# Weight conversions held behind an attention factor, a block of one chunk's input taken from SBUF, and two loads issued later, in a fused attention and two-layer expert kernel

## The chip, the cores and the metric

The kernel runs on one core of a Trainium2 chip. The metric is device time in microseconds (us) of one execution. The core has engines that run side by side, each through its own queue and in that queue's order: TensorE (PE, with its weight loads shown apart as PEld), VectorE (DVE), ScalarE (ACT), GpSimd (POOL), and SyncE (SP), whose queue here issues all the DMA transfers. An instruction that waits holds back everything behind it on its engine.

## What is computed

An attention with a memory term over 4 batches, 8 heads, 576 tokens and a head size of 64 gives 2304 tokens of 512 features; these go through a gated layer and then through a second layer. Cut to what matters:

```python
scores = q @ k.T / 8, causal;  a = softmax(scores);  local = a @ v
q_p = where(q > 0, q, exp(q) - 1) + 1
mem = (q_p @ M_prev) / (q_p @ z_prev + 1e-6)
x = g * mem + (1 - g) * local              # g = sigmoid(beta), per head
x = (sigmoid(x @ w_gate) * (x @ w_val)) @ w_out      # 512 -> 1536 -> 512
h = x @ w_in                                          # 512 -> 2048
out = (h * clip(h + 3, 0, 6) / 6) @ w_out2            # 2048 -> 512
```

All is float32. TensorE multiplies at speed in a shorter format, so the layers split each operand in a high part (a copy into the short format, on ACT) and a low part (the difference, on DVE), and do three products for each one (`mm3`, lines 241 to 245).

## The kernel before

The program has three stages. **Stage A** (`phase_a`) runs the attention and, between its pieces, the first half of the first layer for the first 1872 tokens. The attention is cut in 32 *visits*: visit v is one pair of heads and either rows 0 to 319 of a batch (`rg` 0) or rows 320 to 575 (`rg` 1), in the order of `VISITS`: visits 0 to 3 are the four head pairs of batch 0 with `rg` 0, 4 to 7 the same pairs with `rg` 1, and so on. A visit takes two *steps* of the loop over `t`: step 2v and step 2v+1. In a step TensorE makes a block of scores (L408 up to visit 12, L335 and L336 after it), DVE takes the row maxima out of PSUM (L382, an instruction named `ISA` in orders and `CUSTOM_DVE` in the trace), and ACT takes the exponentials (L432). At a visit's second step `normalize` makes, for v below 8, the factor `nr` (L458, the row sum times the memory term's reciprocal) and `l` (L459, L461). From `nr` POOL writes the memory term's rows into the weights P (L447). Two steps later for v below 4, and three steps later for the others, TensorE transposes the weights (L479), ACT copies the transposes out of PSUM (L481, tile T), and a step after that `pv` (L525) makes the pair's output; ACT copies it out (L534, tile xpr), TensorE spreads `l` (L495), DVE multiplies by it (L536), and the result goes to the DRAM scratch xd (L539 to L541).

The first layer's tokens go in chunks of 312. Chunk 0 needs visits 0 to 3, one head pair (a block of 128 features) from each. `moe_x` (L565) reads the block of a visit back from xd into xc, and ACT and DVE split it (L238, L239, tiles xs). `moe_a` is then a stream of groups of three products (L243 to L245); 4 groups of chunk 0 go into each step, between the scores and the transposes: 48 groups for the gate and value blocks, then 24 for the output.

The weights come as 64-bit numbers and are turned into a high and a low part by a *conversion* (`w_convert`, traced at the end of each odd step from step 7 on; nine of them). One conversion is two ACT instructions (L162, L173) and six on DVE (L163, L164, L165, L167, L168, L174). It waits for its load (tile wst, L151, two buffers) and frees that buffer at L174. From visit 13 on the operands of the scores are split too (L320 on ACT, L321 and L323 on DVE), into a tile that takes over a wst buffer.

TensorE's order is that of the program text. The order on DVE, ACT, POOL and SP is chosen when the program is built, from the builder's own estimate of when each instruction could run; `tc.issue_after(x)` is a way to say that the instructions traced inside it stand behind x on x's engine. PSUM gives the scores, the spread of `l` and the layer's products four buffers in turn (pool `ps_m`), so that a block of scores waits for the maxima that read the buffer's content before.

**Stage B** (`phase_b`) does the rest of the first layer, **stage C** (`phase_c`) the second layer in three chunks of 768 tokens and eight pairs of blocks each. `c_load` (L848) fetches a chunk's input, two transfers, and allocates two tiles for sums of it; it is called in the loop over s, at a chunk's second pair, for the chunk behind it.

Of the kernel before, what the change touches and what calls it, by code (L numbers as in the profile page):

```python
# [9 lines left out]
F32R = mybir.dt.float32r  # L10
# [3 lines left out]
ALU = mybir.AluOpType  # L14
# [6 lines left out]
KT = DM // 128  # L21
NFA = 6
CA = 312
# [27 lines left out]
POST = 8  # L51
# [14 lines left out]
NPAIR = FF2 // 2  # L66
# [18 lines left out]
class Kernel:  # L85
# [162 lines left out]
    def open_attention(self, ctx):  # L248
        self.pa1 = self.pool(ctx, "pa1", 1)
        self.pa2 = self.pool(ctx, "pa2", 2)  # L250
        self.ps_t = self.pool(ctx, "ps_t", 3, space=PSUM)
        self.ps_v = self.pool(ctx, "ps_v", 1, space=PSUM)
        self.attn_consts(self.pa1)
        self.visits, self.done = {}, {}

    def load_visit(self, v):
        if v >= len(VISITS):
# [191 lines left out]
    def normalize(self, v, rg, act):  # L449


        nc = self.nc
        pr = self.visits[v]
        h = pr["pair"][1]
        l, nb = pr["l", rg], len(ROWS[rg])
        c0 = 5 * (h // 2) + 5 - nb
        if v < POST:
            nc.vector.scalar_tensor_tensor(pr["nr"], l, 1e-9, pr["nr"], op0=ALU.add, op1=ALU.mult)  # L458
        nc.vector.scalar_tensor_tensor(l, l, 1e-9, self.a1[:, c0 : c0 + nb], op0=ALU.add, op1=ALU.mult)  # L459
        if v < POST:  # L460
            nc.vector.reciprocal(l, l)  # L461
            return
        nc.vector.reciprocal(l, l)
        for r in range(nb):
            a = self.row(v, rg, r, 64, row_at(rg, r)[1])
            if act or row_at(rg, r)[1] == 640:
                nc.scalar.activation(a, a, AF.Copy, scale=l[:, r : r + 1])
            else:
                nc.vector.tensor_scalar_mul(a, a, l[:, r : r + 1])
# [35 lines left out]
    def pv(self, v, rg):  # L505
        nc = self.nc
        pr = self.visits[v]
# [4 lines left out]
        for g in range(2):  # L512
            if rg == 0:

                o = 64 * g
# [5 lines left out]
        for n in range(last + 1):  # L521
            for g in range(2):
                j, o, c, w = ops[g][n]
                rows = slice(64 * g, 64 * g + 64)
# [8 lines left out]
        x = self.pa2.tile([128, 320], F32, name="xpr", tag="xpr")  # L533
        nc.scalar.copy(x[:, :nt], ps[:, :nt])  # L534
        if v < POST:
            nc.vector.tensor_tensor(x[:, :nt], x[:, :nt], self.spread(v, rg)[:, :nt], op=ALU.mult)  # L536
        dst = self.xd[h // 2, :, b * S + t0 : b * S + t0 + nt]
        if rg == 0:
            nc.sync.dma_start(dst[64:], x[64:, :nt])  # L539
# [20 lines left out]
    def moe_x(self, c, parts=range(KT)):  # L560

        xs = self.xpart
        for k in parts:
            x = self.pm2.tile([128, CA], F32, name="xc", tag="xc")
            self.nc.sync.dma_start(x, self.xd[k, :, c * CA : c * CA + CA])  # L565
            t = self.pm1.tile([128, 2, CA], F32R, name=f"xs{k}", tag=f"xs{k}")
            self.split(t[:, 0], t[:, 1], x, self.nc.scalar, self.nc.vector)
            xs.append((t[:, 0], t[:, 1]))
        if len(xs) == KT:
            self.xnext, self.xpart = (c, xs, self.step), []  # L570

    def moe_a(self, c):

# [39 lines left out]
    def phase_a(self):  # L613
        nc, tc = self.nc, self.tc
# [10 lines left out]
        stream, c = None, 0  # L625
# [30 lines left out]
        t = self.step = 0  # L656
# [6 lines left out]
        while t < nt or tq or vq:  # L663
# [3 lines left out]
            if t < nt:  # L667
                v, rg, i = steps[t]
# [18 lines left out]
            if vq and vq[0][0] <= t:  # L687
                u = vq.pop(0)[1]
                self.pv(*u)
                if u[0] < KT:  # L690
                    first_x.append((t + 1, u[0]))
            if first < w or (tq and tq[0][0] <= t):
                moe(fill // 2)
# [15 lines left out]
                if v + 1 < POST:  # L709
                    self.prep_phi(v + 1)  # L710
            if t >= 7 and t % 2:
                self.w_convert()
            if len(self.wstaged) < 2:
                self.w_load()
            t += 1
# [170 lines left out]
    def phase_c(self):  # L886
        nc, tc = self.nc, self.tc
        ctx = self.ctx
        seq = CSEQ
# [104 lines left out]
        sched.__enter__()  # L994
        add = lambda o, a, b: nc.vector.tensor_tensor(o, a, b, op=ALU.add)  # L995
        for s, (c, j) in enumerate(seq):
            if s % NPAIR == 1 and c + 1 < len(seq) // NPAIR:
                self.c_load(c + 1)
            if s % NPAIR == NPAIR - 2 and c + 1 < len(seq) // NPAIR:
                self.c_sums()  # L1000
# [120 lines left out]
```

## Time and profile before

| | us |
|---|---|
| median of three runs | 1047.61 (1047.41 to 1049.42) |
| the profiled execution | 1048.58, its span 1046.8 |
| PE busy | 1024.6 (98% of the span) |
| DVE busy | 689.7 (66%) |
| ACT busy | 559.0 (53%) |
| POOL busy | 85.8 (8%) |

The span runs from the first instruction to the last; 1.78 us of the profiled execution lie around it. An engine's busy time is the sum of its instructions. The page's picture of 40 slices, 26.2 us each, has TensorE at seven tenths busy in the first two slices and at nine tenths or more in all that follow but the last, DVE at nine tenths or more in the second to the fourth, and the granted TensorE clock at nine tenths or more in all slices but the second.

### The profile page before, as it was taken

The page shows a single profiled execution, that of the slowest core. Times are in us where ns is not written, and L with a number is a line of the kernel's source. Part 1 is how long each engine was busy: PE and PEld are TensorE (multiplying, and loading weights), DVE is VectorE, ACT ScalarE, POOL GpSimd, SP SyncE. Part 2 cuts the span into 40 slices and gives each one's busy share as a digit, 9 for nine tenths or more (in the row PEclk, how much of TensorE's full clock was granted, in tenths as well). Part 3 has the DMA queues.
Part 4 walks back from the last instruction along what each step waited for, and adds up shares of the span by engine and source line. Part 5 has one row for each costly group of instructions (what it writes and reads, how often), then busy time and mean ns, then how long its engine had stood idle before and what let it go on. Part 6 is the DMA issues. An engine that isn't in the chain of part 4 may idle for free.

```text
span 1046.8 us, 16423 instructions
## 1 busy us (share of the span) xinstructions
PE 1024.6 (98%) x5904; PEld 906.8 (87%) x5904; DVE 689.7 (66%) x1634; ACT 559.0 (53%) x1196; POOL 85.8 (8%) x102
## 2 busy tenths in 40 slices
PE   7799999999999999999999999999999999999998
PEld 4467699999899999999888888988988988889887
DVE  6999987676678358888888887743464433743433
ACT  6779797678668544445434443433353333642432
POOL 2112211111111000000000001300002000000000
PEclk9899999999999999999999999999999999999999
DMA  7755564535352334328686876454314542054511
GB/s 228 227 189 181 160 177 132 176 112 154 100 177 74 138 114 149 121 81 298 242 310 233 314 264 247 168 189 147 147 31 162 222 179 83 10 181 161 221 41 60
DMA packets 74032, 172.71 MB, mean 165 GB/s; under 512 B 11232, under 2 KB 48224, under 8 KB 68064
## 3 DMA queue, kind: packets, MB, share of 16 engines
q1 hardware_dynamic: 73952, 171.68, 47.9%
q8 instruction: 46, 0.75, 0.3%
q14 instruction: 34, 0.28, 0.1%
HBM read 130.59 MB, written 41.06 MB: 164 GB/s over the span
## 4 chain that ended last, share of the span: by engine, by line
PE 88%; DVE 4%; DMA 3%; ACT 2%; issue 1%; SPq 1%; POOL 0%; ACTq 0%; DVEq 0%; POOLq 0%
PE acc L942 19%; PE pa L907 9%; PE pb L907 7%; PE g L245 6%; PE g L243 6%; PE g L244 6%; PE m L243 6%; PE m L245 5%; PE m L244 5%; PE pv L525 4%; PE t L479 4%; PE acc L245 3%; PE acc L243 3%; PE acc L244 3%; PE s L336 1%; DMA aux<-in_aux 1%
## 5 line engine op out<-in xcount | busy, mean ns | idle before, releaser
L942 PE MATMUL acc<-wslot,hs 128*128 128x512 f32 x864 | 226.8, 394 | 0.6 <-DVE hs L239 0.6
L942 PEld LDWEIGHTS acc<-wslot,hs 128*128 128x128 f32 x864 | 159.8, 188 | 25.3 <-DVE hs L239 0.9
L907 PE MATMUL pa<-xq,wslot 128*128 128x384 f32 x576 | 116.9, 338 | 0.0
L907 PEld LDWEIGHTS pa<-xq,wslot 128*128 128x128 f32 x576 | 103.8, 188 | 8.2
L245 PE MATMUL g<-xs,wslot 128*128 128x468 f32 (+1 forms) x288 | 106.4, 370 | 0.0
L244 PE MATMUL g<-xs,wslot 128*128 128x468 f32 (+1 forms) x288 | 106.2, 369 | 0.0
L243 PE MATMUL g<-xs,wslot 128*128 128x468 f32 (+1 forms) x288 | 104.1, 369 | 0.0
L243 PE MATMUL m<-xs,wslot 128*128 128x312 f32 x288 | 93.6, 325 | 2.3 <-ACT xs L238 2.3
L432 ACT ACTIVATE P<-P,m 128x192 f32<-128x192 f32 (+4 forms) x144 | 84.0, 586 | 12.9 <-DVE m L382 12.7
L244 PE MATMUL m<-xs,wslot 128*128 128x312 f32 x288 | 88.1, 306 | 0.1
L245 PE MATMUL m<-xs,wslot 128*128 128x312 f32 x288 | 88.1, 306 | 0.0
L907 PE MATMUL pb<-xq,wslot 128*128 128x384 f32 x432 | 87.8, 338 | 0.0
L907 PEld LDWEIGHTS pb<-xq,wslot 128*128 128x128 f32 x432 | 77.8, 188 | 6.2
L995 DVE TENSOR_TENSOR c<-pb,u 128x384 f32<-128x384 f32 x48 | 26.6, 554 | 81.5 <-ACT u L1031 81.5
L919 ACT ACTIVATE r<-c,three 128x384 f32<-128x384 f32 x72 | 44.1, 614 | 62.2 <-DVE c L995 62.2
L239 DVE TENSOR_TENSOR hs<-r,hs 128x384 fp32r<-128x384 f32 x96 | 56.4, 591 | 28.8 <-ACT hs L238 27.4
L481 ACT COPY T<-t 128x512 f32<-128x512 f32 (+2 forms) x128 | 66.3, 544 | 9.3 <-PE t L479 9.2
L479 PE MATMUL t<-ident,P 128*128 128x128 f32 x464 | 66.9, 282 | 4.1 <-POOL P L447 4.1
L162 ACT ACTIVATE wf<-wst 128x512 f32<-128x512 f32 (+1 forms) x59 | 43.9, 745 | 44.4 <-DVE wst L168 36.5
L479 PEld LDWEIGHTS t<-ident,P 128*128 128x128 f32 x464 | 55.4, 145 | 12.8 <-POOL P L447 6.7
L525 PE MATMUL pv<-T,aux 128*64 128x256 f32 (+2 forms) x512 | 62.0, 373 | 2.6 <-ACT T L481 2.6
L238 ACT CAST hs<-r 128x384 fp32r<-128x384 f32 x96 | 48.8, 513 | 29.5 <-DVE r L920 26.9
(118 smaller groups left out, 2074.9 us busy)
## 6 DMA issues: line engine op xcount, KB each, us to landing
wst<-in_wm SPq DMA_DIRECT2D x68, 512.0 KB, 5.7
wslot<-wd SPq DMA_DIRECT2D x30, 1024.0 KB, 4.9
wd<-wslot SPq DMA_DIRECT2D x16, 1024.0 KB, 4.1
wslot<-wd SPq DMA_DIRECT2D x15, 768.0 KB, 6.3
qk<-in_qkd SPq DMA_DIRECT2D x22, 288.0 KB, 3.2
wd<-wslot SPq DMA_DIRECT2D x8, 768.0 KB, 5.7
aux<-in_aux SPq DMA_DIRECT2D x16, 320.0 KB, 3.8
qk<-in_qkd SPq DMA_DIRECT2D x32, 160.0 KB, 2.4
```

What stands on the lines that cost most here:

```text
L238: (ehi.copy if ehi is self.nc.scalar else ehi.tensor_copy)(hi, src)
L239: elo.tensor_tensor(lo, src, hi.bitcast(F32), op=ALU.subtract)
L243: nc.tensor.matmul(out, w[0], x[0], start=first, stop=False)
L244: nc.tensor.matmul(out, w[0], x[1], start=False, stop=False)
L245: nc.tensor.matmul(out, w[1], x[0], start=False, stop=last)
L432: self.nc.scalar.activation(x, x, AF.Exp, bias=vs["m", rg][:, r : r + 1], scale=-1.0, accum_out=vs["l", rg][:, r : r + 1])
L479: nc.tensor.transpose(ps[:, 128 * n : 128 * n + 128], self.row(v, rg, r, 128 * j, 128 * j + 128), self.ident)
L481: nc.scalar.copy(pr["T", rg][:, 512 * k : 512 * k + c], ps[:, :c])
L525: nc.tensor.matmul(ps[rows, o : o + w], pr["v"][:, j, rows], T[:, c : c + w], start=(n == 0), stop=(n == last), skip_group_check=True,)
L907: nc.tensor.matmul(ps[:, :HC], w[:, i, b, cc], x[:, l, k], start=first and k == 0 and n == 0, stop=last and k == 1 and n == 2, skip_group_ ...
L919: nc.scalar.activation(r, src, AF.Relu, bias=self.three)
L942: nc.tensor.matmul(a, h[:, i, cc], w[:, l, f], start=first and f == 0 and n == 0, stop=last and f == 1 and n == 2)
```

## The change

There are three edits.

1. `normalize` keeps a reference to each visit's L458 in a list. A conversion traced at step t is put behind the L458 of visit (t−3)/2, and of visit 7 at the latest: at step 7 that of visit 2, at step 9 that of visit 3, and so on.
2. The block of visit 3, the last that chunk 0 needs, isn't read back from xd. `pv` of visit 3 calls the new `moe_x_here`, which splits the tile xpr itself, in three pieces, as the two halves of its 128 rows hold the tokens at other columns. The block still goes to xd too. The stream of chunk 0 starts one step earlier for it.
3. `c_load` is called at a chunk's fourth pair instead of its second.

```diff
+        self.factor = []
...
         if v < POST:
-            nc.vector.scalar_tensor_tensor(pr["nr"], l, 1e-9, pr["nr"], op0=ALU.add, op1=ALU.mult)
+            self.factor.append(nc.vector.scalar_tensor_tensor(pr["nr"], l, 1e-9, pr["nr"], op0=ALU.add, op1=ALU.mult))
...
+        if v == KT - 1:
+            self.moe_x_here(x)
...
+    def moe_x_here(self, x):
+        k, xs = KT - 1, self.xpart
+        t = self.pm1.tile([128, 2, CA], F32R, name=f"xs{k}", tag=f"xs{k}")
+        for rows, o, c, w in ((slice(0, 64), 64, 0, CA - 64), (slice(0, 64), 0, 256, 64), (slice(64, 128), 0, 0, CA)):
+            hi, lo = t[rows, 0, o : o + w], t[rows, 1, o : o + w]
+            self.split(hi, lo, x[rows, c : c + w], self.nc.scalar, self.nc.vector)
+        xs.append((t[:, 0], t[:, 1]))
+        self.xnext, self.xpart = (0, xs, self.step), []
...
-                if u[0] < KT:
+                if u[0] < KT - 1:
                     first_x.append((t + 1, u[0]))
...
             if t >= 7 and t % 2:
-                self.w_convert()
+                with tc.issue_after(self.factor[min((t - 3) // 2, POST - 1)].ins):
+                    self.w_convert()
...
-            if s % NPAIR == 1 and c + 1 < len(seq) // NPAIR:
+            if s % NPAIR == 3 and c + 1 < len(seq) // NPAIR:
                 self.c_load(c + 1)
```

The built programs differ up to the scores of visit 16, on TensorE up to those of visit 14. Behind that place, each engine's queue holds the same instructions in the same order in both, stage C with its two transfers of `c_load` included. Three places of the part that differs follow. In the rows of the changed kernel the line numbers of attention are higher by one (L459 is L458 of before, L383 is L382), and those of `moe_a` and behind by more.

On DVE, the first conversion. Before, behind the start of visit 2's memory term (L351), its first three instructions alternate with visit 1's factors (L458, L459, L461):

```order
L351 TENSOR_SCALAR phw<-aux 128x320
L163 TENSOR_SCALAR wf<-wf 128x1024
L458 SCALAR_TENSOR_TENSOR nr<-l,nr 128x5
L164 TENSOR_SCALAR wf<-wf 128x1024
L459 SCALAR_TENSOR_TENSOR l<-l,a_120 128x5
L353 SCALAR_TENSOR_TENSOR ph<-aux,phw 128x320
L165 SCALAR_TENSOR_TENSOR wst<-wst,wf 128x1024
```

With the change the first of them stands 27 rows further on, behind visit 2's factor, among the maxima of step 6 (L383) and ahead of the first split of an input block (L239) and the maxima of step 7:

```order
L459 SCALAR_TENSOR_TENSOR nr<-l,nr 128x5
L383 ISA P,m<-s,mask_104 128x64
L383 ISA m 128x1
L163 TENSOR_SCALAR wf<-wf 128x1024
L460 SCALAR_TENSOR_TENSOR l<-l,a_120 128x5
L164 TENSOR_SCALAR wf<-wf 128x1024
L462 RECIPROCAL l<-l 128x5
L165 SCALAR_TENSOR_TENSOR wst<-wst,wf 128x1024
L364 TENSOR_REDUCE nr<-phw 128x5
L537 TENSOR_TENSOR xpr<-xpr,rl 128x320
L239 TENSOR_TENSOR xs_319<-xc,xs_319 128x312
L383 ISA P,m<-s,mask 128x320
```

The conversion now follows the factor that POOL waits for, and what stands behind the conversion waits for it.

On PE, steps 11 and 12. Before, the scores of step 11 (320 and 256 columns) and of step 12 (448) come without a product between, and the chunk's first group follows the transposes of visit 4:

```order
L408 MATMUL s<-qk 128x320 x2
L408 MATMUL s<-qk 128x256 x2
L408 MATMUL s<-qk 128x448 x2
L479 MATMUL t<-ident,P 128x128 x8
L243 MATMUL m<-xs_319,wslot 128x312
L244 MATMUL m<-xs_319,wslot 128x312
L245 MATMUL m<-xs_319,wslot 128x312
L243 MATMUL m<-xs_406,wslot 128x312
```

With the change, two groups stand ahead of the 256 columns and two (the last with visit 3's block, xs_570) behind them:

```order
L409 MATMUL s<-qk 128x320 x2
L243 MATMUL m<-xs_319,wslot 128x312
L244 MATMUL m<-xs_319,wslot 128x312
L245 MATMUL m<-xs_319,wslot 128x312
L243 MATMUL m<-xs_406,wslot 128x312
L244 MATMUL m<-xs_406,wslot 128x312
L245 MATMUL m<-xs_406,wslot 128x312
L409 MATMUL s<-qk 128x256 x2
L243 MATMUL m<-xs_501,wslot 128x312
```

Twelve matmuls moved up by a step; the same number is missing at step 27, where chunk 0 used to end.

On DVE, steps 24 and 25, around the last conversion's last instruction. Before, it stands ahead of the second maximum of step 24 (448 columns), and the first maximum of step 25 (320) comes behind one split of visit 13's operands:

```order
L174 TENSOR_TENSOR wslot<-wst,wslot 128x1024
L382 ISA P,m<-s,mask 128x448
L382 ISA m 128x1
L351 TENSOR_SCALAR phw<-aux 128x256
L239 TENSOR_TENSOR xs_1711<-xc,xs_1711 128x312
L239 TENSOR_TENSOR ha_1413<-th,ha_1413 128x312
L463 RECIPROCAL l<-l 128x5
L321 TENSOR_TENSOR klo<-qk,hi 128x576
L323 TENSOR_TENSOR hi<-qk,hi 64x256
L382 ISA P,m<-s,mask 128x320
```

With the change it stands behind both maxima of step 24 and the five scalings of visit 11's weights, and the first maximum of step 25 behind it and both splits:

```order
L174 TENSOR_TENSOR wslot<-wst,wslot 128x1024
L354 SCALAR_TENSOR_TENSOR ph<-aux,phw 128x256
L239 TENSOR_TENSOR xs_1734<-xc,xs_1734 128x312
L322 TENSOR_TENSOR klo<-qk,hi 128x576
L324 TENSOR_TENSOR hi<-qk,hi 64x256
L364 TENSOR_REDUCE nr<-phw 128x4
L322 TENSOR_TENSOR klo<-qk,hi 128x576
L324 TENSOR_TENSOR hi<-qk,hi 64x256
L366 SCALAR_TENSOR_TENSOR nr<-nr,a_121 128x4
L367 RECIPROCAL nr<-nr 128x4
L383 ISA P,m<-s,mask 128x320
```

The maxima of step 25 moved behind the end of the conversions.

## Rows read from the trace of the kernel before

**Rows 1.** Stretches of the span: length, each engine's busy time, then granted clock.

```profile
core 0: us, PE busy (x) PEld busy (x) DVE busy (x) ACT busy (x) POOL busy (x), PEclk, DMA share, GB/s
15.87:25.00 9.13, 9.13 (x57) 6.25 (x56) 8.92 (x26) 6.72 (x17) 3.08 (x3) 1.00 0.58 186
25.00:58.50 33.50, 26.41 (x170) 16.68 (x169) 30.96 (x94) 25.83 (x64) 7.11 (x9) 0.90 0.68 218
58.50:100.00 41.50, 41.23 (x321) 31.45 (x321) 39.78 (x107) 34.84 (x87) 8.04 (x9) 1.00 0.55 190
100.00:133.00 33.00, 29.71 (x196) 22.16 (x194) 30.14 (x89) 27.01 (x67) 8.43 (x9) 1.00 0.58 164
133.00:1046.80 913.80, 909.55 (x5134) 824.95 (x5132) 572.78 (x1285) 456.42 (x941) 54.48 (x57) 1.00 0.46 160
```

**Rows 2.** Waits of PE: us in total, times, longest.

```profile
PE t L479 <- POOL P L447: 4.1, 3, 2.6
```

**Rows 3.** PE in time: start, length, line, operation, idle before and its releaser.

```profile
23.70 0.59 PE L408 MATMUL s<-qk 64*128 64x192 f32 x4
...
36.27 1.97 PE L479 MATMUL t<-ident,P 128*128 128x128 f32 x8 [2.59 <-POOL P L447]
...
48.98 0.39 PE L243 MATMUL m<-xs,wslot 128*128 128x312 f32 x1
...
49.93 0.60 PE L479 MATMUL t<-ident,P 128*128 128x128 f32 x4
...
53.26 0.41 PE L243 MATMUL m<-xs,wslot 128*128 128x312 f32 x1 [2.30 <-ACT xs L238]
...
57.81 0.70 PE L408 MATMUL s<-qk 64*128 64x256 f32 x2 [0.44 <-DVE m L382]
```

**Rows 4.** DVE in time, from the first conversion to step 13.

```profile
16.11 0.69 DVE L163 TENSOR_SCALAR wf<-wf 128x1024 f32<-128x1024 f32 x1
...
16.83 0.69 DVE L164 TENSOR_SCALAR wf<-wf 128x1024 int32<-128x1024 int32 x1
...
24.44 1.22 DVE L174 TENSOR_TENSOR wslot<-wst,wslot 128x1024 fp32r<-128x1024 f32 x1
25.58 0.35 DVE L382 CUSTOM_DVE_ANT_0 P<-s,mask 128x192 f32<-128x192 f32 x1
...
26.88 0.48 DVE L353 SCALAR_TENSOR_TENSOR ph<-aux,phw 128x320 f32<-128x320 f32 x1
...
35.14 0.16 DVE L458 SCALAR_TENSOR_TENSOR nr<-l,nr 128x5 f32<-128x5 f32 x1
...
55.52 1.22 DVE L165 SCALAR_TENSOR_TENSOR wst<-wst,wf 128x1024 int32<-128x1024 int32 x1
...
57.67 0.48 DVE L382 CUSTOM_DVE_ANT_0 P<-s,mask 128x320 f32<-128x320 f32 x1
```

**Rows 5.** The four DVE instructions of the first conversion on tile wst, one stretch.

```profile
core 0: us, DVE busy (x) ACT busy (x), PEclk, DMA share, GB/s
15.87:25.70 9.83, 4.34 (x4) 2.27 (x2) 1.00 0.61 196
```

**Rows 6.** A stretch at the lower clock, columns as in rows 1.

```profile
36.27:42.00 5.73, 5.73 (x21) 3.12 (x21) 4.68 (x14) 4.21 (x8) 0.63 (x1) 0.50 0.65 195
```

**Rows 7.** Groups on DVE, 15 to 130 us: shapes, count, busy, mean ns.

```profile
L239 DVE TENSOR_TENSOR xs<-xc,xs 128x312 fp32r<-128x312 f32 x6 | 2.9, 478 | 0.4 <-ACT xs L238 0.4
L323 DVE TENSOR_TENSOR hi<-qk,hi 64x256 fp32r<-64x256 f32 x4 | 1.7, 423 | 0.1
L382 DVE CUSTOM_DVE_ANT_0 P<-s,mask 128x64 f32<-128x64 f32 x6 | 1.3, 214 | 0.0
```

**Rows 8.** The first read of a block from xd: SP's issues, then ACT.

```profile
24.90 0.59 SPq L541 DMA_DIRECT2D xd<-xpr  x1
...
28.41 0.33 SPq L565 DMA_DIRECT2D xc<-xd  x1
...
32.49 0.45 ACT L238 CAST xs<-xc 128x312 fp32r<-128x312 f32 x1 [1.07 <-DMA xc<-xd]
```

**Rows 9.** Steps 24 to 27 in time: DVE, then PE.

```profile
115.26 1.22 DVE L174 TENSOR_TENSOR wslot<-wst,wslot 128x1024 fp32r<-128x1024 f32 x1
116.40 0.62 DVE L382 CUSTOM_DVE_ANT_0 P<-s,mask 128x448 f32<-128x448 f32 x1
...
119.23 0.49 DVE L382 CUSTOM_DVE_ANT_0 P<-s,mask 128x320 f32<-128x320 f32 x1
...
123.79 0.47 PE L335 MATMUL s<-hi 128*128 128x448 f32 x1 [0.63 <-DVE m L382]
...
128.95 1.24 PE L525 MATMUL pv<-T,aux 128*64 128x320 f32 x6 [0.55 <-ACT T L481]
```

## The prediction, made before the changed kernel ran

> **What bounds the kernel now.** I read the stretches first [rows 1]. From 133 us to the end TensorE is busy for 909.55 of 913.80 us, and the change leaves every queue from about there on as it was. What can move lies ahead of 133 us, and whatever shift TensorE has there goes through to the end one for one. Ahead of it the table has four stages. In 15.87 to 25 us both PE (9.13 of 9.13) and DVE (8.92) have no room. In 25 to 58.5 us DVE is busy for 30.96 of 33.50 us while PE idles for 7.09: DVE is the bound. In 58.5 to 100 us PE (41.23 of 41.50) is, with DVE close behind (39.78). In 100 to 133 us PE idles for 3.29 us.
>
> Next I read what PE waited for. The largest is POOL's memory rows, 4.1 us in three waits [rows 2], the longest 2.59 us, up to 36.27 us [rows 3]; behind it the granted clock is 0.50, the level of 1.2 GHz, until 42 us [rows 6]. Then come 2.30 us up to 53.26 us for the last input block, which made a round trip through DRAM, and 0.44 us for DVE's maxima of step 13 [rows 3]. Those are what edits 1 and 2 touch. The reader should set them against rows 1: PE's waits are long, but DVE had only 2.54 us to spare in that stage, and a wait of PE that goes is worth nothing beyond what DVE can follow.
>
> **The change part by part, edit 1.** Before, the first conversion runs on DVE from 16.11 to 25.66 us [rows 4]. Its six instructions take 0.69 and 0.69 [rows 4] and 4.34 for the four on wst [rows 5], 5.72 together. In that time the maxima of step 6 aren't to be had anyway, as PE begins their scores at 23.70 [rows 3]: the conversion fills a time in which DVE would else wait for PE. With the change it can't begin before visit 2's factor, which now stands between the maxima of step 6, at about 24.8. PE's queue up to there is unchanged, so the time isn't given back by an earlier start. What moves in is the memory term of visit 3 (0.48) and the maxima of step 6 (two of 0.35 and a smaller one, say 0.9) [rows 4]. So 5.72 − 1.4 = **4.3 us of DVE work leave this stage for the next**.
>
> The next stage is bound by DVE, and takes it up so. Its idle 2.54 us [rows 1] can be filled, as there is now always a conversion waiting: −2.5. At the last maximum of step 13, which ends at 57.67 + 0.48 = 58.15 before [rows 4], the fourth conversion has one L165 less done than before (1.22 [rows 4]): −1.2. Edit 2 adds work: see below, +0.5. That is 4.3 − 2.5 − 1.2 + 0.5 = +1.1 us for the maxima of step 13.
>
> To this comes a new wait. Visit 0's block (L239) now stands ahead of the maxima of step 7 on DVE, and its cast on ACT ahead of the copies of visit 2's transposes. Before, the store to xd ended in an issue at 24.90, the read was issued 3.5 us later, and the cast came 4.1 us behind that, after 1.07 us of idle ACT [rows 8]. With the change the store goes out some 2 us earlier, ahead of a weight load that was in its way, and by the same intervals the cast falls to between 27.8 and 30.4 us, where DVE is ready for it at about 28.3. Bounds 0 and 2.1; the read has no 512 KB load in front of it any more, so I take a value near the lower end, +0.4. Together **+1.5 us at step 13**, bounds +0.8 and +3.2. As PE waited there for DVE before [rows 3], it shifts with it. The waits of PE for POOL don't go as the edit suggests: the factor of visit 3 came at 35.14 [rows 4]; in the new order the whole first conversion and the maxima of steps 7 and 8 still stand ahead of it, which by the same tally puts it at 35.1 to 36.6. So the wait of 2.59 us and the half clock behind it stay; the two shorter waits for POOL go, but under DVE's bound.
>
> From 58.5 to 100 us nothing is won or lost: PE had 0.27 us idle [rows 1]. DVE's conversions lag the maxima by one to three instructions through these steps, at most 0.9 us for PE where a score block waits for a buffer; I take 0, as the next point sets the time anew.
>
> At steps 24 and 25 the order on DVE brings L174 of the last conversion (1.22, at 115.26 [rows 9]) and L168 in front of what follows the second maximum of step 24, and the split of visit 13 needs the buffer that L174 frees. Before, 119.23 − 116.40 = 2.8 us lay between that maximum and the first of step 25 [rows 9]; now L168, five scalings, L174, a split of a block, and two splits of operands do, some 7.8 us. The scores of step 26, which started at 123.79 behind a wait of 0.63 for DVE [rows 9], follow about **1.2 us later**; bounds 0 (if ACT's split isn't waited for and PE has room in its four buffers) and 2.
>
> At step 27 the twelve matmuls are gone that ran earlier: six of them took 49.93 − 48.98 = 0.95 us [rows 3], so **−1.8** for the end of PE's work, and PE's waits for ACT's copies around 128.95 us (0.55 and a smaller one [rows 9]) can close, −0.8 in all. The conversions of weights keep two steps of slack, so no group waits for a weight.
>
> **Edit 2** removes a read of a block from xd and the 2.30 us of PE for it [rows 3]. The stream of chunk 0 can start at step 11, at some 45 us instead of 48.98 [rows 3]; what it is worth at the end is the −1.8 already counted. It turns one pair of instructions into three pairs. The pieces have 248, 64 and 312 columns. The nearest rows are an operation on half the partitions with 256 columns, 423 ns, one with 64 columns, 214, and the whole block, 478 [rows 7]; so DVE pays 423 + 214 + 478 − 478 = 0.64 us at most, and about 0.5 as neighbours overlap by a tenth. ACT pays a like amount beside idle time.
>
> The Trainium skill (Perfetto Trace Analysis, "Optimizing Scalar/DVE Operations") says that an instruction on DVE has a fixed overhead of about 60 ns on SBUF and advises larger operations where the engine is saturated, which speaks against these three pieces. By that overhead alone two more would cost 0.12 us; the half-height row shows that columns count and not rows, and so 0.5.
>
> **Edit 3** does nothing here: the two transfers stand at the same place of SP's queue with the same neighbours, since the builder orders by when an instruction can run. Cost 0, with nothing that hides it.
>
> SP's queue is otherwise re-sorted in stage A: the stores come ahead of loads, and a weight load ahead of some loads of visits. I count 0 for that, with the 0.9 us of the 58.5 to 100 us stage as its upper bound.
>
> **The sum.** +1.5 (step 13), +1.2 (steps 24 to 26), −1.8 (step 27), −0.8 (ACT's copies): +0.1 for PE. ACT, which is fully booked behind step 25, starts its exponentials there with the +1.5 still on it and may hold PE back by up to that; I take +0.4 for it. **+0.5 us.** The profiled execution would be 1048.58 + 0.5 = 1049.1; it lies 0.97 above the median of the runs, so against the median 1047.61 this is **1048.1**. With all lower bounds (+0.8, 0, −1.8, −0.8, 0) it is −1.8, 1045.8; with the upper ones near 1052, but they don't all fall together.
>
> **The rivals.** *The waits go as meant.* If DVE idles less at the start than I reckon, say half of 4.3, step 13 comes 1.1 us early instead of late. With −1.8 at step 27 and the copies closing at 100 us too (−0.9), the end is 3.8 us sooner: 1043.8. For it speaks the size of PE's waits, against it that DVE's queue has no other work ahead of 24.8 us. Chance 0.20.
>
> *Slower: PE is starved and its clock falls a second time.* The first groups at steps 11 and 12 hold one of the four buffers, and the 256 columns of step 11 wait for DVE's product with the spread of visit 3, behind half a conversion. By my tally PE then idles in two pieces of some 1.8 us between 46 and 51 us. The clock went to 0.50 behind an idle of 2.59 us and ran so for 5.73 us [rows 6], worth 2.9 at most; with +0.5 that is +3.3, 1050.9. It decides itself by whether the granted clock falls between 45 and 58 us. Against it: behind the idle of 2.30 us [rows 3] the stage's clock stayed up. Chance 0.27.
>
> The Trainium skill (TensorE: Matmul & The Clock Gate, "HAM oscillation — how this bites in real kernels") says that waits of PE between bursts of matmuls put its clock back to 1.2 GHz again and again. The stretch behind 36.27 us agrees (0.50); by that rule the slower case is the one to expect, by the rows it is open.
>
> **How the numbers follow.** My forecast has 0.50, the faster case 0.20, the slower 0.27, and 0.03 is left for others. A measurement of this kernel can tell about 0.2%, 2.1 us, from no change. The forecast's own range, 1045.8 to 1050.2, lies mostly inside; a few hundredths of it go to either side. So faster 0.20, same 0.52, slower 0.28. The range reaches into both rivals: 1044.2 to 1051.2.
>
> **What would show it.** Right: DVE's busy time in 15.87 to 25 us falls from 8.92 to near 5; the last maximum of step 13 ends at 59 to 60.5 us; the wait for POOL before visit 3's transposes stays near 2.5 us with the clock at 0.50 behind it; the first product starts near 45 us and the wait of 2.30 us is gone; the scores of step 26 start at 125 to 127 us; the rest is as before. Wrong: the end of step 13 at or ahead of 58 us (then faster), a second stretch at 0.50 (then slower), or a difference behind 160 us, where I expect none.

## The result, and the profile after

The changed kernel takes 1058.59 us (median of five runs, 1058.11 to 1059.11), beside 1047.41 us before (1044.59 to 1049.42): a ratio of 1.0107, interval 1.0092 to 1.0122. It is 11 us slower. The forecast was 1048.1 and the range ended at 1051.2, so both are wrong, and so is the slower rival's size. The profiled execution took 1058.26 us with a span of 1056.5; of before, 1046.8.

The stretches of the changed kernel, with the columns of [rows 1]:

```profile
15.87:25.00 9.13, 8.43 (x57) 5.30 (x57) 5.97 (x29) 6.60 (x22) 1.83 (x4) 0.81 0.57 186
25.00:58.50 33.50, 25.86 (x151) 16.45 (x152) 31.73 (x84) 22.88 (x55) 8.83 (x8) 0.80 0.58 183
58.50:100.00 41.50, 41.10 (x315) 31.08 (x315) 38.59 (x108) 35.40 (x85) 9.61 (x10) 1.00 0.56 181
100.00:133.00 33.00, 26.78 (x176) 19.82 (x173) 29.74 (x76) 23.32 (x61) 7.39 (x9) 0.90 0.52 153
...
124.00:128.00 4.00, 3.76 (x15) 3.40 (x17) 3.63 (x8) 2.16 (x3) 0.91 (x1) 0.50 0.08 15
...
47.40:57.40 10.00, 7.62 (x22) 4.64 (x23) 9.56 (x29) 5.53 (x14) 0.10 (x1) 0.50 0.56 192
```

DVE (the third pair) lost 2.95 us of work in the first stretch, from 8.92 to 5.97. PE (the first) lost most from 100 to 133 us: 26.78 us busy, beside 29.71. The granted clock (the fraction after POOL) is down in three stretches where only one was before, and in the last two rows it is at half, 1.2 GHz. What PE waited for:

```profile
PE m L245 <- DVE wslot L174: 5.0, 1, 5.0
PE s L409 <- DVE xpr L537: 3.9, 1, 3.9
PE pv L526 <- ACT T L482: 3.2, 5, 1.2
PE t L480 <- POOL P L448: 2.6, 1, 2.6
```

The waits of [rows 2, 3] that the change meant to take away have partly gone: of 4.1 us for POOL 2.6 are left, and the 2.30 us for the round trip of visit 3's block are gone. Two new ones are larger than both. In time, with the columns of [rows 3]:

```profile
36.38 1.38 PE L480 MATMUL t<-ident,P 128*128 128x128 f32 x8 [2.62 <-POOL P L448]
...
44.37 0.41 PE L243 MATMUL m<-xs,wslot 128*128 128x312 f32 x1 [0.60 <-DVE m L383]
...
49.40 1.22 PE L409 MATMUL s<-qk 64*128 64x256 f32 x2 [3.89 <-DVE xpr L537]
...
59.81 0.81 PE L409 MATMUL s<-qk 64*128 64x320 f32 x4
...
116.92 1.02 PE L409 MATMUL s<-qk 64*128 64x448 f32 x4
...
118.72 0.39 PE L243 MATMUL m<-ha,wslot 128*128 128x312 f32 x1
118.95 0.31 PE L244 MATMUL m<-ha,wslot 128*128 128x312 f32 x1
124.24 0.63 PE L245 MATMUL m<-ha,wslot 128*128 128x312 f32 x1 [4.99 <-DVE wslot L174]
...
127.78 1.44 PE L409 MATMUL s<-qk 64*128 64x320 f32 x4
```

The last wait is the one to look at: the first group of step 24 has its first two products, which read the high part of a weight, and then waits 4.99 us for the low part, which the last conversion's L174 writes. On DVE that instruction stood behind the scalings of visit 11's weights (L470) and ended at 122.98 + 1.21 = 124.19 us:

```profile
121.70 1.35 DVE L470 TENSOR_SCALAR P<-P,l 128x320 f32<-128x320 f32 x3
122.98 1.21 DVE L174 TENSOR_TENSOR wslot<-wst,wslot 128x1024 fp32r<-128x1024 f32 x1
```

How far each kernel is behind the kernel before at the start of a step's scores (us, from the profiled executions; the variants are those of the experiments below):

| step (start before) | whole change | edit 1 | edit 2 | edit 2, later stream | first conversion free | first two conversions free | last conversion first |
|---|---|---|---|---|---|---|---|
| 11 (44.09) | −1.1 | −0.4 | −0.2 | −2.7 | −3.3 | −3.3 | −1.9 |
| 13 (54.26) | +5.6 | +4.3 | +3.0 | −1.9 | +0.1 | +0.2 | +4.7 |
| 21 (98.56) | +4.6 | +3.9 | +2.4 | −2.4 | +2.6 | −0.7 | +3.8 |
| 24 (112.00) | +4.9 | +3.1 | +2.2 | −2.7 | +5.7 | 0.0 | +4.1 |
| 25 (116.03) | +11.8 | +3.1 | +4.3 | −2.7 | +5.7 | +6.5 | +8.5 |
| 26 (123.79) | +9.4 | +3.1 | +2.7 | −1.7 | +2.7 | +4.2 | +5.6 |
| 28 (133.56) | +9.4 | +2.5 | +1.9 | −0.9 | +1.8 | +4.0 | +4.2 |

A minus means ahead. From step 13 to step 26 the kernels whose stream starts a step earlier have done four groups more than the kernel before, some 1.8 us of work. Each column is one profiled execution. The ratios below come from several, and executions of the kernel before alone spread from 1045.12 to 1051.23 us, so a column's end and its ratio can differ by 2 or 3 us. Differences in us "above before" are worked out from the ratios unless medians or the trace are named.

The whole change loses its time in two places, between steps 11 and 13 and between steps 24 and 25, and from step 28 on next to nothing moves any more: +9.4 there, and +9.7 at the end of the span.

### The profile page after: what moved, and what is told of

Its sections match the earlier page's. It is cut to its first block, busy times and chain, and to the rows that moved or that the text cites. A ratio compares the mean times of both kernels' runs of the same rounds, so it can differ in the third digit from the quotient of the medians.

```text
span 1056.5 us, 16424 instructions
## 1 busy us (share of the span) xinstructions
PE 1026.7 (97%) x5904; PEld 907.6 (86%) x5904; DVE 692.7 (66%) x1636; ACT 560.1 (53%) x1198; POOL 87.2 (8%) x102
## 4 chain that ended last, share of the span: by engine, by line
PE 89%; DVE 5%; DMA 2%; ACT 2%; issue 1%; SPq 1%; ACTq 0%; DVEq 0%
PE acc L957 19%; PE pa L922 9%; PE pb L922 7%; PE g L245 6%; PE g L243 6%; PE g L244 6%; PE m L243 6%; PE m L245 5%; PE m L244 5%; PE pv L526 4%; PE t L480 4%; PE acc L245 3%; PE acc L243 3%; PE acc L244 3%; PE s L336 1%
## 5 line engine op out<-in xcount | busy, mean ns | idle before, releaser
L433 ACT ACTIVATE P<-P,m 128x192 f32<-128x192 f32 (+4 forms) x144 | 83.8, 586 | 11.8 <-DVE m L383 11.6
L239 DVE TENSOR_TENSOR hs<-r,hs 128x384 fp32r<-128x384 f32 x96 | 56.2, 589 | 28.8 <-ACT hs L238 27.4
```

Of the source, the lines that this page charges most:

```text
L239: elo.tensor_tensor(lo, src, hi.bitcast(F32), op=ALU.subtract)
L433: self.nc.scalar.activation(x, x, AF.Exp, bias=vs["m", rg][:, r : r + 1], scale=-1.0, accum_out=vs["l", rg][:, r : r + 1])
```

## The experiments

**The three edits, one at a time.** Edit 1 alone leaves out `moe_x_here` and the new place of `c_load`; edit 2 alone leaves out the hold on the conversions and the new place of `c_load`; edit 3 alone is that new place, one line. Edit 1 alone, against the whole change (cut):

```diff
-        if v == KT - 1:
-            self.moe_x_here(x)
...
-                if u[0] < KT - 1:
+                if u[0] < KT:
```

> Edit 1 alone: the conversions are held behind the factors, the block of visit 3 is read back from xd, and chunk 0's stream starts at step 12. Theory A (the wait of 3.9 us at step 11 comes from edit 1: in the order that it gives, ACT's cast of visit 2's block, which waits for a read from DRAM, stands ahead of ACT's copy of visit 3's output): the wait of PE at step 11 for DVE's product with the spread stays, 3.5 to 5 us, with the clock at 0.50 behind it; no wait for a weight at step 24; 1052 to 1054 us. Theory B (it comes from edit 2, whose two groups at step 11 hold buffers of the scores): no such wait, 1047 to 1049 us.

Measured: 1.0026 (1.0015 to 1.0036), 1051.23 us against 1048.01. Theory A's wait was there and theory A's time was not:

```profile
49.80 1.22 PE L409 MATMUL s<-qk 64*128 64x256 f32 x2 [3.99 <-DVE xpr L537]
```

So the wait at step 11 belongs to edit 1, but edit 1 costs only 2.7 us, less than the wait alone.

> Edit 2 alone: the conversions are where the builder put them before, visit 3's block is split from SBUF and chunk 0's stream starts at step 11. Theory A: no wait at step 11 over 1 us, and the last conversion's last instruction stands ahead of the maxima of step 24, so the wait for a weight there is under 1 us: the 2.3 us for the block's round trip are won, 1044.5 to 1047 us. Theory B: the wait of 3.9 us at step 11 is there, 1050 to 1053 us.

Measured: 1.0007 (0.9995 to 1.0019): no change. The wait at step 11 has gone (0.8 us for all products with the spread), as theory A said, but nothing was won. In the new order PE waits 3.63 us for POOL before visit 3's transposes, where it waited 2.59 before, and the wait for the weight at step 24 was not under 1 us:

```profile
118.36 0.41 PE L245 MATMUL m<-ha,wslot 128*128 128x312 f32 x1 [1.78 <-DVE wslot L174]
```

The wait for the last conversion is there with edit 2 alone, if smaller.

> Edit 3 alone: the builder gives the same order on every engine as for the kernel before. 1047.4 us, within 0.1% of before; any difference over that would say that the place of the call acts through something other than the order.

Measured: 1.0003 (0.9990 to 1.0016). Edit 3 does nothing, as forecast. The edits one by one add up to 2.7 + 0.7 + 0.3 = 3.7 us of 11.2; the other 7.5 arise only when edits 1 and 2 come together.

**Both edits, but the stream of chunk 0 a step later.**

```diff
-        self.xnext, self.xpart = (0, xs, self.step), []
+        self.xnext, self.xpart = (0, xs, self.step + 1), []
```

> Both edits of the attention, but chunk 0's stream starts at step 12 as before. Theory C (the wait of 5.0 us at step 24 comes from the stream's earlier start: the group that needs the last converted weights stands a step earlier, ahead of their conversion): no wait for a weight over 0.5 us, the wait at step 11 stays, 1051 to 1054 us. Theory D (it comes from DVE's backlog of some 5 us, whichever step the stream starts at): a wait for a weight of 3 us or more stays at step 24 or 25, 1056 to 1059 us.

Measured: 1.0049 (1.0035 to 1.0062), 5.1 us above before and some 6 us under the whole change. No wait for a weight is left among PE's: theory C. The wait at step 11 is still 4.0 us. The run has a loss of its own, which makes its size hard to read: at step 18 DVE stands 3.95 us for a load of another visit. With it PE is 7.6 us late at step 24, more than the whole change, but still only 7.3 at step 28, as no product waits for a weight between the two.

```profile
86.64 0.33 DVE L352 TENSOR_SCALAR phw<-aux 128x320 f32<-128x320 f32 x1 [3.95 <-DMA aux<-in_aux]
```

**Step 11 repaired.** In the changed kernel, visit 3's copy out of PSUM (L535) stood on ACT behind the cast of visit 2's block, which waited 1.62 us for its read from DRAM, a conversion's first instruction and an exponential:

```profile
45.67 0.45 ACT L238 CAST xs<-xc 128x312 fp32r<-128x312 f32 x1 [1.62 <-DMA xc<-xd]
46.02 1.13 ACT L162 ACTIVATE wf<-wst 128x1024 f32<-128x1024 f32 x1
47.05 0.66 ACT L433 ACTIVATE P<-P,m 128x448 f32<-128x448 f32 x1
47.61 0.19 ACT L433 ACTIVATION_READ_ACCUMULATOR P<-P,m 128x1 f32 x1
47.71 0.41 ACT L535 COPY xpr<-pv 128x320 f32<-128x320 f32 x1
```

The repair puts visit 2's split and the third conversion behind that copy and behind L537:

```diff
+            with self.tc.issue_after(copied.ins), self.tc.issue_after(spread.ins):
+                self.split(s[:, 0], s[:, 1], xc, nc.scalar, nc.vector)
...
+                    if t == 11:
+                        for x in self.made:
+                            hold.enter_context(tc.issue_after(x.ins))
                     self.w_convert()
```

> The whole change, but at steps 10 and 11 ACT's copy of visit 3's output stands ahead of the cast of visit 2's block and of the third conversion's first ACT instruction, and DVE's product with the spread ahead of the split of that block and of the third conversion. Theory A (the place on ACT and DVE makes the wait of 3.9 us at step 11): the wait falls under 1 us, the clock stays at 1.00 between 45 and 58 us, the scores of step 13 start at 54 to 56.5 us instead of 59.8; and if the wait at step 24 is a loss of its own, 1052 to 1055 us. Theory F (DVE's backlog is the one bound, and PE's two waits are only where it shows): what is won at step 11 is lost again at step 24, where the wait for the weight grows from 5.0 to 8 us or more; 1057 to 1059 us.

Measured: 1.0100 (1.0082 to 1.0118), as slow as the whole change. It is not a clean test, as the wait at step 11 fell only to 2.6 us: the copy now ran at 45.95, but L537 stood on DVE behind visit 4's memory term, until 48.51. Step 13 started at 58.91, 0.9 us earlier. That was lost at step 24, where the last conversion ended at 127.20 us, 3.0 later than in the whole change. PE waited for it twice, 3.47 us for its high part and 4.26 for its low part:

```profile
122.10 0.63 PE L243 MATMUL m<-ha,wslot 128*128 128x312 f32 x1 [3.47 <-ACT wslot L173]
...
127.25 0.63 PE L245 MATMUL m<-ha,wslot 128*128 128x312 f32 x1 [4.26 <-DVE wslot L174]
```

So far as it goes, this is theory F: what PE gains ahead of a conversion that doesn't come sooner, it waits for later. As the builder's new order also made the conversion later, the run doesn't show it cleanly.

**Step 24 repaired.** The maxima of step 24 and the scalings of visit 11 stand behind the last conversion, which is traced ahead of them:

```diff
-                self.score_part(v, i, 0, first)
+                with tc.issue_after(self.converted.ins) if t == 24 else ExitStack():
+                    self.score_part(v, i, 0, first)
...
+                    if t == 23:
+                        self.w_convert()
+                    with tc.issue_after(self.converted.ins) if t == 23 else ExitStack():
+                        self.normalize(v, rg, 5 <= t < 22)
...
-            if t >= 7 and t % 2:
+            if 7 <= t < 23 and t % 2:
```

> The whole change, but the maxima of step 24 and the five scalings of visit 11 stand behind the last conversion on DVE instead of ahead of its last instruction. Theory C (PE waits at step 24 for that instruction, which stands behind 3 us of other work): the wait for the weight falls from 5.0 to between 1 and 2.5 us, 1054.5 to 1057 us. Theory F: the maxima, now 2.4 us later, are waited for instead at steps 25 and 26; 1058 to 1060 us.

Measured: 1.0047 (1.0031 to 1.0063), 1053.47 us, 5.1 us less than the whole change by the medians (6.3 by the ratios) and more than expected. The conversion ended 3.1 us sooner and the wait fell to 2.63 us:

```profile
119.42 1.63 DVE L174 TENSOR_TENSOR wslot<-wst,wslot 128x1024 fp32r<-128x1024 f32 x1
...
121.10 0.49 PE L245 MATMUL m<-ha,wslot 128*128 128x312 f32 x1 [2.63 <-DVE wslot L174]
```

The maxima, which came 2.3 us later than in the whole change, were not waited for at steps 25 and 26. In the table the run is 5.2 us ahead of the whole change at step 28. Of these 0.8 were there at step 24, 2.4 are the shorter wait, and the clock gives most of the rest: it came back to full speed in this run between 124 and 127 us (0.89 in that stretch), and in the whole change only at some 129.

> Both edits of order of the two runs ahead of this one together. Two losses of their own: 1049 to 1052 us, with no wait over 1.5 us at step 11 and under 3 us at step 24. Theory F: 1056 us or more.

Measured, with both repairs: 1.0056 (1.0040 to 1.0071). Neither theory's number: no better than the repair of step 24 alone, though step 13 started 1.7 us sooner than in that run. The wait at step 11 was still 2.6 us, not under 1.5. At step 24 PE, 1.2 us sooner than in that run, met a last conversion that ended 0.4 us later (121.47), and waited 2.0 us for its high part and 2.0 for its low part, instead of 2.6 in all. So the two places aren't losses of their own: what was taken out of the wait at step 11 was waited for again at step 24.

**Edit 2 with the later stream,** the diff of one line above on edit 2 alone:

> Edit 2 alone with chunk 0's stream starting at step 12 as before. The twelve matmuls stay where they were, so no group waits for a weight (0 to 0.3 us instead of 1.8). If the 2.30 us for the block's round trip were worth something by themselves: 1045 to 1046.5 us. If DVE sets the pace of that stage anyway: 1047 to 1048.5 us, with waits of PE for DVE or POOL in its place.

Measured: 1.0017 (1.0004 to 1.0029). No wait for a weight is left. By its time this is the second case, but the trace shows that the round trip was worth something: without it PE is 1.9 us ahead of the kernel before at step 13 and 2.7 at step 24 (table). At step 26 it then waits for a maximum that DVE brings only 1.8 us sooner than before:

```profile
122.12 0.44 PE L336 MATMUL s<-hi 128*128 128x448 f32 x1 [3.34 <-DVE m L383]
```

Of the 2.7 us 0.9 are left at step 28 and nothing at the end of the span (1047.1). So what edit 2 won in one stage was lost in the next, in an order of the builder's that was new there too.

**Which hold counts.** A kernel that holds the first conversion alone and leaves the other eight free is, on all five queues, the same program, row for row, as the whole change. So it is the first one; these two free it, and the first two:

```diff
-                with tc.issue_after(self.factor[min((t - 3) // 2, POST - 1)].ins):
+                with tc.issue_after(self.factor[min((t - 3) // 2, POST - 1)].ins) if t > 7 else ExitStack():
```

> The whole change without the hold on the first conversion alone: it runs where it ran before, from 16 us on; the other eight stay held behind their factors. Theory G (the loss starts with the 3 us that DVE idles at 16 to 25 us, which leave every conversion 6 to 8 us late, until the last one is waited for at step 24): DVE is busy for 8.5 us or more of 15.87 to 25 us, the last conversion ends before 119 us instead of 124.2, PE's wait for it is under 1 us, 1047 to 1050.5 us. Theory H (the holds on the later conversions or the order at step 24 do it): a wait of 3 us or more for the last conversion stays, 1054 us or more.

Measured: 1.0027 (1.0014 to 1.0039), 8.4 us less than the whole change (7.4 by the medians). DVE is busy for 8.56 us of 15.87 to 25, the last conversion ends at 114.4 us, and no group waits for it:

```profile
15.87:25.00 9.13, 9.07 (x56) 6.55 (x57) 8.56 (x26) 6.81 (x18) 3.08 (x3) 1.00 0.59 189
```

These are theory G's signs, with a time 0.7 us above its range. But the table shows more. At step 24 this run is later than the whole change, 5.7 us behind the kernel before against 4.9. The difference to the whole change arises there: without the wait for the weight it is still 5.7 behind at step 25, where the whole change is 11.8 behind, and 1.8 at step 28 against 9.4. What it doesn't show is whether DVE's time or the place of L174 did it, as L174 now also stands ahead of the maxima of step 24. For the second run `t > 9` stands in place of `t > 7`:

> The whole change without the hold on the first two conversions. From the fourth conversion on DVE's order is that of the whole change, with the last conversion's last instruction behind the maxima of step 24 and the five scalings. Theory G: DVE's 3 us are back, the wait at step 24 falls from 5.0 to between 1 and 3 us, 1050 to 1054 us. Theory H' (the place in the queue makes the wait, whenever the conversions run): it stays at 4 to 5.5 us, 1055 us or more.

Measured: 1.0061 (1.0048 to 1.0075), 1053.79 us, and the wait stays at 4.62 us: theory H'. Here the scores of step 24 start when they do in the kernel before (0.0 in the table), and yet the wait is there, as the order at step 24 puts the five scalings (L470) and a maximum ahead of L174. So the order at step 24 and the earlier stream are enough to make the wait. DVE, behind the second maximum of step 24:

```profile
114.61 1.22 DVE L168 CUSTOM_DVE_ANT_0 wst<-wst,wf 128x2048 uint16<-128x2048 uint16 x1
...
115.94 0.47 DVE L470 TENSOR_SCALAR P<-P,l 128x64 f32<-128x64 f32 x2
...
116.43 1.36 DVE L470 TENSOR_SCALAR P<-P,l 128x320 f32<-128x320 f32 x3
117.71 1.21 DVE L174 TENSOR_TENSOR wslot<-wst,wslot 128x1024 fp32r<-128x1024 f32 x1
```

and PE, for which it is 4.62 us and the half clock behind them:

```profile
118.98 0.63 PE L245 MATMUL m<-ha,wslot 128*128 128x312 f32 x1 [4.62 <-DVE wslot L174]
```

```profile
114.40:119.00 4.60, 0.02 (x1) 0.03 (x1) 4.60 (x12) 2.77 (x8) 0.72 (x1) 0.81 0.16 39
119.00:123.50 4.50, 4.50 (x17) 3.67 (x17) 3.87 (x9) 2.16 (x3) 0.97 (x2) 0.50 0.23 49
```

**DVE's time by itself.** The kernel before, with the first conversion's L163 six times:

```diff
-        nc.vector.tensor_scalar(w, w, HI_MIN, HI_MAX, op0=ALU.max, op1=ALU.min)
+        for _ in range(6 if not self.w else 1):
+            nc.vector.tensor_scalar(w, w, HI_MIN, HI_MAX, op0=ALU.max, op1=ALU.min)
```

> The kernel before, with the first conversion's clamp (L163, 0.69 us) done six times instead of once: 3.45 us more work for DVE at 16 to 25 us, nothing else new; the builder orders DVE, ACT and SP anew around it. Theory F (DVE sets the pace of 16 to 58 us, and what it loses there reaches the end): 1050 to 1052 us, about what edit 1 alone costs (2.7). Rival (PE's idle time and the slack of the conversions take it up): within 1 us of before.

Measured: 1.0098 (1.0084 to 1.0112). Both theories are far off: 3.45 us of work for DVE cost 10.3 us. PE waits 5.79 us for POOL at step 9 and 4.06 us for the product with the spread at step 11, both with the clock at half behind them:

```profile
39.82 1.97 PE L480 MATMUL t<-ident,P 128*128 128x128 f32 x8 [5.79 <-POOL P L448]
...
53.06 1.22 PE L409 MATMUL s<-qk 64*128 64x256 f32 x2 [4.06 <-DVE xpr L537]
```

```profile
40.00:44.00 4.00, 4.00 (x17) 2.69 (x19) 3.48 (x9) 1.74 (x4) 0.98 (x1) 0.50 0.26 77
...
53.00:59.60 6.60, 6.01 (x15) 3.15 (x15) 6.60 (x19) 3.68 (x7) 0.19 (x1) 0.50 0.47 127
```

The builder's new order is part of this price, and the run can't part the two. It speaks against the rival, that slack would take up work of DVE at 16 to 25 us, but puts no price on that work alone.

**PE's clock by itself.** The kernel before, with sixteen transposes of the identity ahead of visit 3's transposes:

```diff
+        for _ in range(16 * (v == KT - 1 and k == 0)):
+            nc.tensor.transpose(ps[:, :128], self.ident, self.ident)
```

> The kernel before with sixteen transposes of the identity, which nobody reads, ahead of visit 3's transposes at step 8, in the 2.6 us in which PE waits there for POOL; the builder orders DVE and ACT anew around them. Theory K (PE's half clock of 5.7 us behind that wait costs up to 2.9 us): the clock stays at 1.00 from 36 to 42 us, the end comes 1.5 to 3 us earlier, 1045 to 1046.5 us. Theory F (DVE sets the pace of this stage, so that PE's clock there costs nothing): 1047.5 to 1049.5 us with the clock at 1.00 all the same.

Measured: 1.0038 (1.0025 to 1.0050), slower. (By the count of the table the wait lies in step 9.) The clock stayed up, and PE came to step 11 at 41.63 us instead of 44.09:

```profile
36.27:42.00 5.73, 5.25 (x41) 3.10 (x39) 4.86 (x14) 4.58 (x10) 0.00 (x0) 1.00 0.87 245
42.00:58.50 16.50, 12.58 (x60) 8.23 (x59) 16.50 (x47) 11.69 (x26) 4.05 (x4) 0.90 0.60 198
```

In the second row DVE has no idle time at all (16.50 of 16.50), and PE is busy for 12.58. Of the 2.46 us 0.86 are left at step 13 (53.40 against 54.26). The rest went into waits of PE, 1.24 us for DVE's product with the spread and 2.45 for the cast of the block read back from DRAM. The end doesn't price the clock. By step 21 the run is 2.9 us behind the kernel before, in an order that was new here as well, with new waits of PE for DVE (1.26 us at 71 us, 1.18 at 93). So a full clock gained PE some 0.9 us by step 13 in this run, and what the half clock costs at the end isn't shown.

No variant beat the kernel before.

## Why the prediction was wrong, step by step

**The slack of the conversions: the step that failed.** The prediction said that the conversions "keep two steps of slack, so no group waits for a weight", and read no row for it. The rows were there. In the kernel before, the last conversion's L174 starts at 115.26 and ends at 116.48 [rows 9], and the first product that reads its result is the low part's of step 25's first group:

```profile
119.63 0.41 PE L243 MATMUL m<-ha,wslot 128*128 128x312 f32 x1
119.88 0.31 PE L244 MATMUL m<-ha,wslot 128*128 128x312 f32 x1
120.03 0.31 PE L245 MATMUL m<-ha,wslot 128*128 128x312 f32 x1
```

That is 3.55 us of slack, less than one step. Edit 2 moves this group up by four places, to the first of step 24, whose third product stood here:

```profile
114.18 0.30 PE L245 MATMUL m<-ha,wslot 128*128 128x312 f32 x1
```

So with nothing else changed the group would come 116.48 − 114.18 = 2.3 us ahead of its weight. The wait in each run is that 2.3, plus the delay of the conversion's end (L174, start and length), less the delay of step 24's scores. Edit 2's L174 is this row; the others are shown above:

```profile
117.10 1.21 DVE L174 TENSOR_TENSOR wslot<-wst,wslot 128x1024 fp32r<-128x1024 f32 x1
```

| kernel | end of the last L174 | its delay | delay of step 24 | worked out | measured |
|---|---|---|---|---|---|
| edit 2 alone | 118.31 | 1.8 | 2.2 | 1.9 | 1.78 |
| whole change | 124.19 | 7.7 | 4.9 | 5.1 | 4.99 |
| first two conversions free | 118.92 | 2.4 | 0.0 | 4.7 | 4.62 |
| last conversion first | 121.05 | 4.6 | 4.1 | 2.8 | 2.63 |

With the first conversion free the same sum is negative (an end at 114.39 and scores 5.7 late), and there is no wait. The prediction's sum had 0 for this term. Measured, steps 24 to 25 took 127.78 − 116.92 = 10.86 us, beside 4.03 before. Of the 6.8 more 4.99 are the wait and some 1.8 the half clock behind it (124.24 to 127.78 at half speed). About 2.4 came back by step 26.

**Beside the sum.** At step 28 the whole change is 9.4 us late in its trace, 8.9 more than the +0.5 of the forecast. Of the 8.9, 3.4 were there at step 24 (+4.9, where the sum had +1.5), and 3.3 came between steps 24 and 26 (+4.5, where it had +1.2). Another 2.6 are the −1.8 and the −0.8, which didn't come. ACT's +0.4 was not seen as a term of its own. So the wait for the weight is the step that failed, but not the only term that was off.

**Edit 1's tally for DVE: right in kind, too small.** DVE's busy time in the first stretch fell to 5.97 us ("near 5"): 2.95 us of work left it, where the sum had 4.3. But the sum let DVE win back 2.5 in the next stage, and it won 0.8: its idle time in 25 to 58.5 us went from 2.54 [rows 1] to 33.50 − 31.73 = 1.77 us. Its idle pieces there are waits for others, with the conversion queued behind them: 0.63 us for POOL at 28 us, 0.62 for ACT's cast of visit 2's block at 46 us. So having a conversion waiting at all times doesn't fill DVE, as it waits in the same queue. The last maximum of step 13, forecast to end at 59 to 60.5 us, ended at 61.71 + 0.48 = 62.2, 4.0 later than before where +1.5 had been forecast. The lower bound of that term, +0.8, doesn't follow from its own parts either, which give 1.1 + 0. The sum had no term for the wait of 3.89 us at step 11, which the prediction kept for its slower rival. By itself the hold cost 2.7 us.

**Steps 24 to 26: +1.2 was forecast,** for the maxima of step 25 behind the end of the conversions, and the scores of step 26 at 125 to 127 us. They came at 133.16. The queue that the prediction quoted for it, L174 behind both maxima and five scalings, was the right one; it asked what stands behind L174 on DVE and not who on PE waits for L174 itself. The delay that it priced didn't act: the first maximum of step 25 stood 0.69 us idle for PE, which was late from its own wait.

```profile
129.25 0.49 DVE L383 CUSTOM_DVE_ANT_0 P<-s,mask 128x320 f32<-128x320 f32 x1 [0.69 <-PE s L409]
```

**Step 27's −1.8 and ACT's −0.8 didn't show.** The delay was 9.4 us at step 26 and 9.4 at step 28. ACT, whose split of operands waited 1.24 us for a load, brought the copy of the transposes late instead:

```profile
139.91 0.86 PE L526 MATMUL pv<-T,aux 128*64 128x256 f32 x6 [1.16 <-ACT T L482]
```

**The slower rival's mechanism came, and it wasn't the price.** As it said, the scores of step 11 waited for the product with the spread, in one piece of 3.89 us instead of two of 1.8. The clock fell to half at 47.4 us, within the wait, and stayed there for 8.0 us behind it (49.40 to 57.40), not 5.7. The rival was given 3.3 us (2.9 + 0.5 is 3.4) and a chance of 0.27. But edit 1 alone has the same wait and ends 2.7 us late, and with 1.3 to 1.5 us of it taken away no run got faster. Nor is DVE the only cause: the rival blamed half a conversion, and the trace shows ACT's copy behind a read from DRAM as well.

**What was right.** PE's wait for POOL before visit 3's transposes stayed (2.62 us, forecast near 2.5) with the clock at half behind it, if for less long (0.70 on average from 36.38 to 42 us, beside 0.50 in [rows 6]); the first product came at 44.37 us (near 45), and the wait of 2.30 us went; edit 3 did nothing; behind 160 us nothing moved.

**What stays open.** The hold costs 2.7 us alone, edit 2 0.7, and 7.5 come of the two together. By the traces the wait at step 24 with its half clock is worth 4 to 7.6 us at step 28. The run that was level with before up to step 24 is 4.0 behind there (3.9 in the span; 5.4 by the medians, 6.4 by the ratios). The repair that shortened the wait gave 5.2 back, and the run with the first conversion free, which has no such wait, is 7.6 ahead of the whole change. The rest isn't parted: every variant also got a new order from the builder, with small waits of its own.

## What to carry to other kernels

When a stream of work is moved up, everything that it reads is due that much earlier: list its producers (weights as well as inputs), and for each subtract the producer's end from the new reader's start, from rows. A wait that is seen on an engine that isn't the bound is worth what the bound can follow. Here 0.9 of the 2.5 us that a full clock won at step 11 were left at step 13, and what was taken out of the wait at step 11 was waited for again at step 24. So follow a gain from stage to stage: the round trip's was there until step 24 and gone by the end. And a hold on one instruction, where a builder sorts the rest by its estimates, is a change of the whole order behind it: the hold on the first of nine conversions alone made the program of all nine.

## What the runs showed of the hardware

The granted clock needn't be alike in two executions with the same order on every engine. Edit 3's program has the order of the kernel before; its profile has the clock at 0.81 in a stretch where [rows 1] have 1.00. Its span is 1044.3 us, 2.5 less, within what executions of the kernel before spread by, so the lower clock there cost nothing that can be seen:

```profile
15.87:25.00 9.13, 8.82 (x60) 5.79 (x59) 8.93 (x26) 7.30 (x19) 3.08 (x3) 0.81 0.64 203
```

So the 0.81 of the changed kernel's first stretch needn't come of the change. In the changed kernel each of the waits of 2.62, 3.89 and 4.99 us had the half clock behind it; the wait of 1.78 us in edit 2's run had not, with a clock of 1.00 from 118 to 124 us. The Trainium skill (TensorE: Matmul & The Clock Gate, "HAM oscillation — how this bites in real kernels") says that waits between bursts bring the lower clock back again and again, and the changed kernel agrees: 0.50 at 47.4 to 57.4 us and at 124 to 128. In the run with sixteen transposes the clock stayed at 1.00 from 36 to 42 us, and 0.86 of the 2.46 us that PE won by it were left at step 13.
